# Inputs of the next block as separate tasks, low parts of the FFN on VectorE, early banks that change roles, and a longer Sinkhorn step

## The chip, the cores and the metric

The kernel runs on one core of a Trainium2 chip. The metric is the device time of one execution in microseconds; lower is better. TensorE (PE) does the matmuls, VectorE (DVE), ScalarE (ACT) and GpSimd (POOL) the elementwise work, and SyncE (SP) issues nearly all DMAs.

## What is computed

Three stages, all in float32: attention with a local mask in four heads and a strided mask in the other four, then a mixture of experts whose gate is normalised by eight Sinkhorn rounds, then an FFN with a sigmoid activation.

```python
scores = scale * q @ k.T                # 4 x 8 heads, 576 tokens, 64 wide
attn = softmax(where(mask, scores, -1e9))
x = (attn @ v) as (2304, 512)
P = exp(x @ w_gate - max)               # 8 experts
for _ in range(8):
    P /= P.sum(1, keepdims=True) + 1e-9
    P /= P.sum(0, keepdims=True) + 1e-9
    P *= N / E
for e in range(8):
    out += P[:, e:e+1] * (max(x @ w1[e], 0) @ w2[e])    # 512 -> 1024 -> 512
h = out @ w_in                          # 512 -> 2048
y = (h * sigmoid(1.702 * h)) @ w_out    # 2048 -> 512
```

## The kernel before

**Precision.** Every float32 operand of the large matmuls is split into a high part (rounded by a copy on ACT) and a low part (the difference), and a product is the sum of high x high, low x high and high x low: three matmuls in the fast fp32r form.

**Blocks, units, pieces.** The 2304 tokens are three blocks of 768. `PHASES` (line 145) gives the order of the passes: moe block 0, moe 1, FFN 0, moe 2, FFN 1, FFN 2. A pass consists of units (`UNITS`), each a slice of 256 hidden columns: 32 units for a moe pass, 8 for an FFN pass, 120 in all; they are numbered 0 to 119. In a unit the up projection is done by the seven products of a Strassen scheme (`PRODUCTS`, line 39) instead of eight: the inputs are X11, S1, S2, X12, S3, S4, X22, where S1 to S4 are sums of quarters of the block's input. Each product is six matmuls of 384 columns and accumulates in PSUM banks A, B and C. The down projection of the unit before is six tiles (`tile_down`) of six matmuls of 512 columns. The work is emitted in pieces that alternate: product 0, down tile 0, product 1, down tile 1, and so on; the last product (X22) has no tile behind it. A unit has 13 pieces (`PPU`), and piece k of unit i is `piece_at(i, k)`; product m is piece 2m. Small tasks are hung behind pieces in the table `side`. The order is written out by hand, and each engine runs its own instructions in that order.

**After the products** (`product_and_after`, `activate`, lines 580 to 632). ACT copies partial sums out of a bank, DVE adds them to another bank, and each of four quarters "11", "22", "12", "21" is activated. In the moe ACT writes the high part hh with a Relu, and DVE writes the low part hl (line 589). In the FFN ACT computes the sigmoid (594), DVE multiplies (595), ACT copies to hh (596), and POOL writes the low part hl (599). The low part is returned as `rest` and called behind the next down tile (`after`); only for the last quarter, "21", it is called at once while the attention is still running. The down tile needs hh in its first two and hl in its third matmul (lines 646 to 648). Its result y is added to the accumulator on DVE (lines 659 to 675).

**Banks.** While the attention runs (`late` is empty), A, B and C have one bank each, as the attention holds the others; the last products of a unit (X22) and the first of the next one (X11) both use A. From `early.close()` on each of the three has two banks in turn (`open_bank`, line 117). Units 0 to about 8 run between the steps of the attention; the first piece starts at about 71 us.

**Inputs of a block** (`combine`, line 292; `plan_inputs`, line 320). For each of the seven products of the next pass it issues, where there is one, the sum S1 to S4, then ACT's copy to the high part (316) and the low part (317). Product 0's is issued in the last unit but one of the pass before (behind its piece 8), product m's behind piece 2m - 1 of the last unit. Sums and low parts run on POOL, for a pass over block 0 on DVE. S1 and S3 share one buffer, S2 and S4 another, and S2 is computed from S1, S4 from S2. The tiles xc have eight buffers, one more than a pass needs.

**Weights.** For passes over block 0 (units 0 to 31 and 64 to 71) the weights of each unit are summed on POOL (`sums_w1`, 185 to 187) and split by ACT and POOL (`split_w1`, 204, 205; `split_w2`, 217, 218) one unit ahead, and kept in DRAM; the other passes load them split. POOL is free of that work there. The FFN weights are decoded from 64-bit words on DVE and POOL (`decode`, 254 to 266) as side tasks between the gate and unit 60.

**Gate.** The first twelve units (three experts) don't wait for the gate: their outputs are parked in DRAM and joined later by DVE (line 689), from unit 14 on. The gate's steps (`gate_steps`, line 545) are hung behind consecutive pieces once the attention has been issued: each of eight iterations is a row half on DVE (`sinkhorn_rows`, which ends with the partial column sums, 532), an empty step, and a column half (`sinkhorn_cols`), which begins with a matmul over partitions on PE (536) and goes on on DVE.

Of the kernel before, what the change touches and what calls it, by code (L numbers as in the profile page):

```python
# [8 lines left out]
F32 = mybir.dt.float32  # L9
F32R = mybir.dt.float32r  # L10
U32 = mybir.dt.uint32
AF = mybir.ActivationFunctionType
ALU = mybir.AluOpType
AX = mybir.AxisListType

P = 128
# [9 lines left out]
NH = 384  # L26
BT = 2 * NH
# [11 lines left out]
PRODUCTS = (  # L39
    ("X11", "W11", "A", True, False),  # L40
    ("S1", "T1", "C", True, False),
    ("S2", "T2", "A", False, False),
    ("X12", "W21", "B", True, True),
    ("S3", "T3", "A", False, False),
    ("S4", "W22", "C", False, True),
    ("X22", "T4", "A", False, True),
)
# [4 lines left out]
def strided_attention_moe_ffn(  # L52
# [13 lines left out]
    nc = tc.nc  # L66
    B, NPAIR, _, _, S = qk.shape
# [20 lines left out]
    stp = ctx.enter_context(tc.tile_pool(name="stp", bufs=1))  # L88
# [6 lines left out]
    ps = ctx.enter_context(tc.tile_pool(name="ps", bufs=1, space=bass.MemoryType.PSUM))  # L95
# [17 lines left out]
    late = []  # L113
    bank = {}
    turn_of = defaultdict(int)

    def open_bank(b):
        turn_of[b] += 1
        pool, tag = (late[0], b + "2") if late and turn_of[b] % 2 else (ps, b)
        bank[b] = pool.tile([P, 512], F32, tag=tag, name="p" + b)  # L120
        return bank[b]

# [8 lines left out]
    def f(t):  # L131
        return t.bitcast(F32)


    side = defaultdict(list)
# [9 lines left out]
    PHASES = [("moe", 0), ("moe", 1), ("ffn", 0), ("moe", 2), ("ffn", 1), ("ffn", 2)]  # L145
# [11 lines left out]
    def piece_at(unit, k):  # L157
        return unit * PPU + k
# [130 lines left out]
    xc = {}  # L289
    xin = {}  # L290

    def combine(ph, m):

        x = xin[ph]
        X11, X12 = x[:, 0:2, 0:NH], x[:, 2:4, 0:NH]
        X21, X22 = x[:, 0:2, NH:BT], x[:, 2:4, NH:BT]
        if ("sa", ph) not in xin:
            xin["sa", ph] = stp.tile([P, 2, NH], F32, tag="sa", name="sa")
            xin["sb", ph] = stp.tile([P, 2, NH], F32, tag="sb", name="sb")
        sa, sb = xin["sa", ph], xin["sb", ph]  # L300

        v = nc.gpsimd if ph and PHASES[ph][1] else nc.vector
        what = PRODUCTS[m][0]
        if what == "S1":
            v.tensor_tensor(out=sa, in0=X21, in1=X22, op=ALU.add)
        elif what == "S2":
            v.tensor_tensor(out=sb, in0=sa, in1=X11, op=ALU.subtract)
        elif what == "S3":
            v.tensor_tensor(out=sa, in0=X11, in1=X21, op=ALU.subtract)
        elif what == "S4":  # L310
            v.tensor_tensor(out=sb, in0=X12, in1=sb, op=ALU.subtract)
        src = {"X11": X11, "X12": X12, "X22": X22, "S1": sa, "S2": sb, "S3": sa, "S4": sb}[what]
        if ph == 0 and not xc:
            xc.update({(0, n): xcp.tile([P, 2, 2, NH], F32R, tag="xc", name="xc") for n in range(NPR)})
        t = xc[0, m] if ph == 0 else xcp.tile([P, 2, 2, NH], F32R, tag="xc", name="xc")
        nc.scalar.activation(out=t[:, 0], in_=src, func=AF.Copy)  # L316
        v.tensor_tensor(out=t[:, 1], in0=src, in1=f(t[:, 0]), op=ALU.subtract)  # L317
        xc[ph, m] = t

    def plan_inputs():  # L320
        for ph in range(1, len(PHASES)):
            last = FIRST_UNIT[ph] - 1
            side[piece_at(last, 0) - 5].append(lambda ph=ph: combine(ph, 0))
            for m in range(1, NPR):
                side[piece_at(last, 2 * m - 1)].append(lambda ph=ph, m=m: combine(ph, m))


    xblk = [tok.tile([P, KD, BT], F32, tag="tok", name="x") for _ in range(NB)]
# [146 lines left out]
    for n, p in enumerate(pairs):  # L475
        if n > 0:
            i = at[pairs[n - 2]][-1] if n > 1 else -1
# [18 lines left out]
    def gate_logits(blk):  # L496

        pl = spare_bank([P, TB, Q], "pl")
        xv = xblk[blk].rearrange("p k (t c q) -> p k c t q", c=P // Q, q=Q)
        for k in range(KD):  # L500
            for c in range(P // Q):
                nc.tensor.matmul(
                    out=pl[c * Q : (c + 1) * Q],
                    lhsT=wgr[:, k, :],
                    rhs=xv[:, k, c],
                    start=(k == 0),
                    stop=(k == KD - 1),
                )
        lt = stp.tile([P, TB * Q], F32, tag="sg", name="lt", bufs=2)
        nc.vector.transpose(lt, pl.rearrange("p t q -> p (t q)"))  # L510
        nc.vector.tensor_copy(pr[:, blk * TB : (blk + 1) * TB, :], lt.rearrange("p (t q) -> p t q", q=Q)[:, :, :E])
# [33 lines left out]
    def gate_steps():  # L545
        steps = [lambda blk=blk: gate_logits(blk) for blk in range(1, NB)] + [gate_max]
        steps += [lambda: None] * 3 + [gate_exp]
        for _ in range(SINKHORN):
            steps += [sinkhorn_rows, lambda: None, sinkhorn_cols]
        return steps  # L550


# [4 lines left out]
    def product(i, k):  # L557
        ph, kind, blk, n = UNITS[i]
        _, _, b, opens, ends = PRODUCTS[k]
        if opens:  # L560
            open_bank(b)
        o = bank[b][:, :NH]
        w, x = w1.pop((i, k)), xc[ph, k]
        todo = [(kk, hw, hx) for kk in range(2) for hw, hx in ((0, 0), (0, 1), (1, 0))]
        for m, (kk, hw, hx) in enumerate(todo):
            nc.tensor.matmul(  # L566
                out=o,
                lhsT=w[:, hw, kk * P : (kk + 1) * P],
                rhs=x[:, hx, kk, :],
                start=opens and m == 0,  # L570
                stop=ends and m == len(todo) - 1,
                skip_group_check=True,
            )

    def copy_of(b):
        t = cp.tile([P, NH], F32, tag="c", name="c")
        nc.scalar.activation(out=t, in_=bank[b][:, :NH], func=AF.Copy)  # L577
        return t

    def activate(i, q, src):  # L580

        hh = hp.tile([P, NH], F32R, tag="hh" + q, name="hh" + q, bufs=2 if q == "22" else 1)
        hl = hp.tile([P, NH], F32R, tag="hl" + q, name="hl" + q, bufs=2 if q == "22" else 1)
        hid[i, q] = (hh, hl)
        if UNITS[i][1] == "moe":
            nc.scalar.activation(out=hh, in_=src, func=AF.Relu)  # L586

            def rest():
                nc.vector.scalar_tensor_tensor(  # L589
                    out=hl, in0=src, scalar=0.0, in1=f(hh), op0=ALU.max, op1=ALU.subtract  # L590
                )
        else:
            sg = stp.tile([P, NH], F32, tag="sg", name="sg", bufs=2)
            nc.scalar.activation(out=sg, in_=src, func=AF.Sigmoid, scale=1.702)
            nc.vector.tensor_tensor(out=sg, in0=src, in1=sg, op=ALU.mult)
            nc.scalar.activation(out=hh, in_=sg, func=AF.Copy)  # L596

            def rest():
                nc.gpsimd.tensor_tensor(out=hl, in0=sg, in1=f(hh), op=ALU.subtract)  # L599

        return rest

    def add(t, b, to):
        o = bank[to][:, :NH]
        nc.vector.tensor_tensor(out=o, in0=bank[b][:, :NH], in1=t, op=ALU.add)  # L605
        return o

    def product_and_after(i, k):

        product(i, k)  # L610
        x = PRODUCTS[k][0]
        if x == "X11":
            snap["a"] = copy_of("A")
        elif x == "S1":
            snap["c"] = copy_of("C")
        elif x == "S2":
            snap["u"] = copy_of("A")
        elif x == "X12":
            return activate(i, "11", add(snap["a"], "B", "B"))
        elif x == "S3":  # L620
            if late:
                o = open_bank("B")[:, :NH]
                nc.vector.tensor_tensor(out=o, in0=bank["A"][:, :NH], in1=snap["c"], op=ALU.add)
                return activate(i, "22", o)
            return activate(i, "22", add(snap["c"], "A", "B"))
        elif x == "X22":
            rest = activate(i, "21", bank["A"][:, :NH])
            if late:
                return rest
            rest()  # L630
        elif x == "S4":
            return activate(i, "12", add(snap["u"], "C", "C"))

# [113 lines left out]
    with tc.manual_schedule():  # L747
# [19 lines left out]

        plan_weights()
        plan_inputs()
        plan_kept()  # L770
        plan_turns()
# [45 lines left out]
        dp = ctx.enter_context(tc.tile_pool(name="dp", bufs=1, reuse_waits="tile"))  # L817
        g = done[0]
        steps = gate_steps()
        assert g + len(steps) + 2 < piece_at(WAITING * UPE + 1, 0), (g, len(steps))  # L820
        for n, s in enumerate(steps):
# [85 lines left out]
```

## Time and profile before

| | before |
|---|---|
| device time, median of 3 runs | 2095.91 us (2093.35 to 2096.3) |
| the profiled execution: its own time | 2096.66 us |
| its span, first to last instruction | 2094.9 us |
| PE busy | 2028.2 us, 97% |
| DVE busy | 1254.8 us, 60% |
| ACT busy | 707.6 us, 34% |
| POOL busy | 699.4 us, 33% |
| mean granted TensorE clock | 0.989 of 2.4 GHz |

Busy shares are means over stages with different loads. A matmul is recorded with a modelled end, so PE's busy time is an upper figure; what a stage loses is better seen in the distance between like pieces of the chain of waits and in the waits by name. In a windows row the columns are the stretch and its length, the busy time of each engine with its number of instructions, the granted clock, the share of the DMA engines and their rate.

### The profile page before, as it was taken

What the parts mean: (1) busy time and instruction counts of PE and PEld (TensorE: products, weight loads), DVE (VectorE), ACT (ScalarE), POOL (GpSimd) and SP (SyncE); (2) the same over time, 40 slices, a digit from 0 to 9 for tenths busy, and PEclk for the clock granted to TensorE, in tenths of its full rate; (3) what the DMA queues carried; (4) which work ended last, traced back from release to release, by engine and by line L of the source; (5) the groups of instructions that cost most, each with busy time, mean ns of one, the idle gap of its engine ahead of it and who ended that gap; (6) DMA issues with size and microseconds to landing.
All of it is one profiled execution on the core that took longest, in us unless ns stands there. A gap on an engine that the chain in (4) does not pass through costs nothing.

```text
span 2094.9 us, 30326 instructions
## 1 busy us (share of the span) xinstructions
PE 2028.2 (97%) x10538; PEld 1781.8 (85%) x10538; DVE 1254.8 (60%) x2214; ACT 707.6 (34%) x1735; POOL 699.4 (33%) x705
## 2 busy tenths in 40 slices
PE   9799989999998999999999998999999999999899
PEld 6577778888887888888988897798888888898788
DVE  6766577888776666666665643444544545544444
ACT  5555434344443222222222554222222222333332
POOL 3555547777776000000000688100000000423522
PEclk9899999999999999999999999999999999999999
DMA  5467558888886667667666575566556566556553
GB/s 180 154 207 269 203 206 303 313 300 306 290 291 213 206 212 219 207 223 223 215 214 195 202 249 203 191 181 197 177 180 199 178 179 198 172 178 184 172 190 132
DMA packets 185289, 445.52 MB, mean 213 GB/s; under 512 B 21040, under 2 KB 21168, under 8 KB 184368
## 3 DMA queue, kind: packets, MB, share of 16 engines
q1 hardware_dynamic: 184848, 443.12, 64.1%
q8 instruction: 84, 1.38, 0.3%
q14 instruction: 69, 0.57, 0.1%
q10 hardware_dynamic: 288, 0.46, 0.1%
HBM read 310.33 MB, written 133.17 MB: 212 GB/s over the span
## 4 chain that ended last, share of the span: by engine, by line
PE 85%; DVE 6%; POOL 5%; issue 2%; ACT 1%; DMA 1%; POOLq 0%; SPq 0%; DVEq 0%; ACTq 0%
PE pA L566 21%; PE y L648 15%; PE y L646 14%; PE y L647 14%; PE pC L566 11%; PE pB L566 5%; POOL xc L317 1%; PE sc L365 1%; PE idle_out L755 1%; PE av L434 1%; DVE hl L589 1%; POOL w L205 1%; PE pt L416 1%; DVE acc L665 1%; DVE acc L689 1%
## 5 line engine op out<-in xcount | busy, mean ns | idle before, releaser
L665 DVE SCALAR_TENSOR_TENSOR acc<-y,pr,acc 128x512 f32<-128x512 f32 x486 | 364.1, 749 | 445.1 <-PE y L648 442.6
L646 PE MATMUL y<-w,hh 128*128 128x512 f32 x1440 | 569.0, 395 | 22.1 <-ACT hh L596 9.9
L648 PE MATMUL y<-w,hl 128*128 128x512 f32 x1440 | 574.4, 399 | 5.5 <-DVE hl L589 4.4
L566 PE MATMUL pA<-xc,w 128*128 128x384 f32 x2880 | 566.3, 337 | 10.8 <-DVE hl L589 6.1
L647 PE MATMUL y<-w,hh 128*128 128x512 f32 x1440 | 570.5, 396 | 0.0
L566 PEld LDWEIGHTS pA<-xc,w 128*128 128x128 f32 x2880 | 514.2, 189 | 46.2 <-DVE hl L589 7.8
L648 PEld LDWEIGHTS y<-w,hl 128*128 128x128 f32 x1440 | 271.0, 188 | 68.2 <-DVE hl L589 6.7
L646 PEld LDWEIGHTS y<-w,hh 128*128 128x128 f32 x1440 | 271.7, 189 | 62.5 <-ACT hh L596 15.6
L647 PEld LDWEIGHTS y<-w,hh 128*128 128x128 f32 x1440 | 271.2, 188 | 33.7
L566 PE MATMUL pC<-xc,w 128*128 128x384 f32 x1440 | 296.1, 340 | 0.0
L566 PEld LDWEIGHTS pC<-xc,w 128*128 128x128 f32 x1440 | 260.6, 191 | 21.4 <-issue 0.6
L586 ACT ACTIVATE hh<-pB 128x384 fp32r<-128x384 f32 x192 | 94.4, 492 | 395.3 <-DVE pB L605 228.1
L577 ACT ACTIVATE c<-pA 128x384 f32<-128x384 f32 x240 | 117.6, 490 | 258.9 <-PE pA L566 258.9
L265 POOL TENSOR_TENSOR x<-x,r 128x512 f32<-128x512 f32 x32 | 41.4, 1294 | 413.9 <-DVE r L264 392.2
L317 POOL TENSOR_TENSOR xc<-z,xc 128x768 fp32r<-128x768 f32 x6 | 11.1, 1849 | 481.2 <-ACT xc L316 479.1
L599 POOL TENSOR_TENSOR hl<-sg,hh 128x384 fp32r<-128x384 f32 x96 | 97.8, 1019 | 172.1 <-ACT hh L596 148.0
L675 DVE TENSOR_TENSOR acc<-y,acc 128x512 f32<-128x512 f32 x126 | 86.5, 687 | 105.9 <-PE y L648 105.7
L566 PE MATMUL pB<-xc,w 128*128 128x384 f32 x720 | 145.7, 336 | 0.0
L205 POOL TENSOR_TENSOR w<-sums,w 128x256 fp32r<-128x256 f32 x160 | 125.2, 786 | 59.6 <-ACT w L204 52.3
L566 PEld LDWEIGHTS pB<-xc,w 128*128 128x128 f32 x720 | 128.2, 188 | 11.1 <-issue 0.5
L218 POOL TENSOR_TENSOR w<-raw,w 128x512 fp32r<-128x512 f32 x80 | 104.9, 1311 | 78.0 <-ACT w L217 69.4
L577 ACT ACTIVATE c<-pC 128x384 f32<-128x384 f32 x120 | 59.0, 492 | 189.7 <-PE pC L566 189.7
(112 smaller groups left out, 1978.5 us busy)
## 6 DMA issues: line engine op xcount, KB each, us to landing
w<-s1moe SPq DMA_DIRECT2D x448, 256.0 KB, 2.7
w<-s2moe SPq DMA_DIRECT2D x128, 512.0 KB, 3.7
s1moe<-w SPq DMA_DIRECT2D x224, 256.0 KB, 3.3
s2moe<-w SPq DMA_DIRECT2D x64, 512.0 KB, 4.1
w<-s1ffn SPq DMA_DIRECT2D x112, 256.0 KB, 2.7
raw<-wa SPq DMA_DIRECT2D x32, 512.0 KB, 4.6
raw<-wb SPq DMA_DIRECT2D x32, 512.0 KB, 5.4
w<-s2ffn SPq DMA_DIRECT2D x32, 512.0 KB, 3.6
```

The source lines that it names most:

```text
L205: nc.gpsimd.tensor_tensor(out=t[:, 1, :], in0=src, in1=f(t[:, 0, :]), op=ALU.subtract)
L218: nc.gpsimd.tensor_tensor(out=t[:, 1, :], in0=src, in1=f(t[:, 0, :]), op=ALU.subtract)
L265: lambda: nc.gpsimd.tensor_tensor(out=x, in0=x, in1=f(r), op=ALU.add),
L566: nc.tensor.matmul(out=o, lhsT=w[:, hw, kk * P : (kk + 1) * P], rhs=x[:, hx, kk, :], start=opens and m == 0, stop=ends and m == len(todo) - 1,
L577: nc.scalar.activation(out=t, in_=bank[b][:, :NH], func=AF.Copy)
L586: nc.scalar.activation(out=hh, in_=src, func=AF.Relu)
L599: nc.gpsimd.tensor_tensor(out=hl, in0=sg, in1=f(hh), op=ALU.subtract)
L646: nc.tensor.matmul(out=y, lhsT=hh[:, c], rhs=w[:, 0], start=(m == 0), stop=False)
L647: nc.tensor.matmul(out=y, lhsT=hh[:, c], rhs=w[:, 1], start=False, stop=False)
L648: nc.tensor.matmul(out=y, lhsT=hl[:, c], rhs=w[:, 0], start=False, stop=(m == 1))
L665: nc.vector.scalar_tensor_tensor(out=a, in0=y, scalar=p, in1=a, op0=ALU.mult, op1=ALU.add)
L675: nc.vector.tensor_tensor(out=a, in0=y, in1=a, op=ALU.add)
```

## The change

Four edits.

1. `open_bank` takes the unit's number. While the attention runs, A and B change roles in odd units. The low part of quarter "21" is no longer called at once there, but behind the next down tile, as everywhere else.
2. `combine` is divided into `input_sum`, `input_high` and `input_low`, each with the engine as an argument, and `plan_inputs` hangs them apart: S1 and S2 of the next pass behind pieces 6 and 8 of the last unit but one, on POOL; the high part of product 0 behind piece 9 and its low part behind piece 10 of that unit; high and low part of product m behind piece 2m - 1 of the last unit as before; S3 and S4 behind pieces 2 and 4 of the last unit. Before a pass over block 0 (FFN 0) low parts 1, 3, 5 and S3, S4 are on DVE; before the pass that follows one over block 0 (moe 1, moe 2) low parts 0, 3, 6 are on DVE; all others are on POOL. The inputs of pass 0 are made as before.
3. The low part hl of the FFN's activations goes from POOL to DVE.
4. A Sinkhorn iteration has two empty steps between its halves instead of one, so 4 pieces instead of 3; the gate has 39 steps instead of 31, and the decode starts after them.

```diff
-    def open_bank(b):
+    def open_bank(b, i):
         turn_of[b] += 1
-        pool, tag = (late[0], b + "2") if late and turn_of[b] % 2 else (ps, b)
+        pool, tag = ps, b
+        if late and turn_of[b] % 2:
+            pool, tag = late[0], b + "2"
+        elif not late and i % 2:
+            tag = {"A": "B", "B": "A", "C": "C"}[b]
...
+    SUMS = {"S1": "sa", "S2": "sb", "S3": "sa", "S4": "sb"}
+    def input_sum(ph, m, eng):
...
+        what = PRODUCTS[m][0]
         if what == "S1":
-            v.tensor_tensor(out=sa, in0=X21, in1=X22, op=ALU.add)
+            eng.tensor_tensor(out=sa, in0=q["X21"], in1=q["X22"], op=ALU.add)
...
+    def input_high(ph, m):
...
+        nc.scalar.activation(out=t[:, 0], in_=input_of(ph, m), func=AF.Copy)
         xc[ph, m] = t
+    def input_low(ph, m, eng):
+        t = xc[ph, m]
+        eng.tensor_tensor(out=t[:, 1], in0=input_of(ph, m), in1=f(t[:, 0]), op=ALU.subtract)
...
     def plan_inputs():
+        v, g = nc.vector, nc.gpsimd
         for ph in range(1, len(PHASES)):
             last = FIRST_UNIT[ph] - 1
-            side[piece_at(last, 0) - 5].append(lambda ph=ph: combine(ph, 0))
+            shared = PHASES[ph][1] == 0
+            low_v = (1, 3, 5) if shared else (0, 3, 6) if PHASES[ph - 1][1] == 0 else ()
...
+            put(last - 1, 6, input_sum, ph, 1, g)
+            put(last - 1, 8, input_sum, ph, 2, g)
+            put(last - 1, 9, input_high, ph, 0)
+            put(last - 1, 10, input_low, ph, 0, v if 0 in low_v else g)
             for m in range(1, NPR):
-                side[piece_at(last, 2 * m - 1)].append(lambda ph=ph, m=m: combine(ph, m))
+                put(last, 2 * m - 1, input_high, ph, m)
+                put(last, 2 * m - 1, input_low, ph, m, v if m in low_v else g)
+                if m in (1, 2):
+                    put(last, 2 * m, input_sum, ph, m + 3, v if shared else g)
...
-            steps += [sinkhorn_rows, lambda: None, sinkhorn_cols]
+            steps += [sinkhorn_rows, lambda: None, lambda: None, sinkhorn_cols]
...
             def rest():
-                nc.gpsimd.tensor_tensor(out=hl, in0=sg, in1=f(hh), op=ALU.subtract)
+                nc.vector.tensor_tensor(out=hl, in0=sg, in1=f(hh), op=ALU.subtract)
...
         elif x == "X22":
-            rest = activate(i, "21", bank["A"][:, :NH])
-            if late:
-                return rest
-            rest()
+            return activate(i, "21", bank["A"][:, :NH])
```

## Rows read from the trace of the kernel before

**Rows 1.** Page: span; busy time of each engine, share, instructions.

```profile
span 2094.9 us, 30326 instructions
PE 2028.2 (97%) x10538; PEld 1781.8 (85%) x10538; DVE 1254.8 (60%) x2214; ACT 707.6 (34%) x1735; POOL 699.4 (33%) x705
```

**Rows 2.** Chain of waits in order of time: start us, us, what.

```profile
624.46 2.08 PE pA L566 x12
...
679.52 2.08 PE pA L566 x12
...
1152.44 2.08 PE pA L566 x12
...
1188.96 2.08 PE pA L566 x12
...
1269.88 2.08 PE pA L566 x12
...
1330.85 2.08 PE pA L566 x12
...
1800.05 2.08 PE pA L566 x12
...
1832.78 2.08 PE pA L566 x12
...
1929.34 2.08 PE pA L566 x12
...
1972.15 2.08 PE pA L566 x12
```

**Rows 3.** Waits by name, whole span: who waited for whom, us, times, longest.

```profile
ACT xc L316 <- POOL sa L309: 18.2, 4, 6.2
...
PE y L646 <- ACT hh L586: 8.2, 3, 6.2
```

**Rows 4.** Waits of PE and of its weight loads, 95 to 265 us.

```profile
PE pA L566 <- DVE hl L589: 6.1, 8, 1.2
...
PEld pA L566 <- DVE hl L589: 7.8, 8, 1.5
```

**Rows 5.** Waits of PE, 265 to 325 us.

```profile
PE pc L536 <- DVE sk L532: 6.2, 6, 2.1
```

**Rows 6.** Busy time in four stretches: Sinkhorn, moe 0, FFN 0, moe 2.

```profile
280.00:322.00 42.00, 35.83 (x172) 30.43 (x171) 34.86 (x100) 13.11 (x33) 23.16 (x27) 0.96 0.62 225
...
531.00:640.00 109.00, 109.00 (x545) 97.93 (x544) 79.05 (x127) 47.09 (x113) 81.84 (x87) 1.00 0.82 282
...
1190.00:1271.00 81.00, 81.00 (x416) 72.90 (x416) 38.99 (x66) 45.65 (x106) 70.50 (x81) 1.00 0.71 244
...
1332.00:1785.00 453.00, 453.00 (x2261) 407.11 (x2260) 227.66 (x377) 99.87 (x203) 0.00 (x0) 1.00 0.60 187
```

**Rows 7.** Groups by line: shapes, count | busy us, mean ns | idle before.

```profile
L599 POOL TENSOR_TENSOR hl<-sg,hh 128x384 fp32r<-128x384 f32 x96 | 97.8, 1019 | 172.1 <-ACT hh L596 148.0 <-PE pA L566 23.9
...
L218 POOL TENSOR_TENSOR w<-raw,w 128x512 fp32r<-128x512 f32 x80 | 104.9, 1311 | 78.0 <-ACT w L217 69.4 <-DVE pB L623 8.5
...
L317 POOL TENSOR_TENSOR xc<-sb,xc 128x768 fp32r<-128x768 f32 x8 | 14.9, 1863 | 7.6 <-ACT xc L316 7.6
...
L316 ACT ACTIVATE xc<-sb 128x768 fp32r<-128x768 f32 x12 | 10.1, 843 | 33.7 <-POOL sb L311 13.0 <-POOL sb L307 12.2 <-DVE sb L311 5.0
...
L595 DVE TENSOR_TENSOR sg<-pB,sg 128x384 f32<-128x384 f32 x48 | 26.7, 557 | 45.7 <-ACT sg L594 45.0 <-POOL w L205 0.6
...
L317 DVE TENSOR_TENSOR xc<-x,xc 128x768 fp32r<-128x768 f32 x3 | 2.9, 958 | 1.9 <-ACT xc L316 1.8
...
L311 DVE TENSOR_TENSOR sb<-x,sb 128x768 f32<-128x768 f32 x1 | 3.7, 3694 | 0.0
```

**Rows 8.** Groups of DVE by line, 531 to 640 us (moe 0).

```profile
L264 DVE SCALAR_TENSOR_TENSOR r<-r,u 128x512 f32<-128x512 uint32 x5 | 4.4, 871 | 0.0
```

**Rows 9.** Groups of DVE by line, 762 to 1138 us (moe 1).

```profile
L264 DVE SCALAR_TENSOR_TENSOR r<-r,u 128x512 f32<-128x512 uint32 x15 | 10.2, 682 | 0.0
```

More of the change, by code (lines that the diff above doesn't have):

```diff
@@ L290, in strided_attention_moe_ffn, with quarters, input_of @@
     xin = {}
-    def combine(ph, m):
+    SUMS = {"S1": "sa", "S2": "sb", "S3": "sa", "S4": "sb"}
+    def quarters(ph):
         x = xin[ph]
-        X11, X12 = x[:, 0:2, 0:NH], x[:, 2:4, 0:NH]
-        X21, X22 = x[:, 0:2, NH:BT], x[:, 2:4, NH:BT]
+        return {"X11": x[:, 0:2, 0:NH], "X12": x[:, 2:4, 0:NH], "X21": x[:, 0:2, NH:BT], "X22": x[:, 2:4, NH:BT]}
+    def input_sum(ph, m, eng):
+        q = quarters(ph)
         if ("sa", ph) not in xin:
-            xin["sa", ph] = stp.tile([P, 2, NH], F32, tag="sa", name="sa")
-            xin["sb", ph] = stp.tile([P, 2, NH], F32, tag="sb", name="sb")
+            for n in ("sa", "sb"):
+                xin[n, ph] = stp.tile([P, 2, NH], F32, tag=n, name=n)
         sa, sb = xin["sa", ph], xin["sb", ph]
-        v = nc.gpsimd if ph and PHASES[ph][1] else nc.vector
         what = PRODUCTS[m][0]
         if what == "S1":
-            v.tensor_tensor(out=sa, in0=X21, in1=X22, op=ALU.add)
+            eng.tensor_tensor(out=sa, in0=q["X21"], in1=q["X22"], op=ALU.add)
         elif what == "S2":
-            v.tensor_tensor(out=sb, in0=sa, in1=X11, op=ALU.subtract)
+            eng.tensor_tensor(out=sb, in0=sa, in1=q["X11"], op=ALU.subtract)
         elif what == "S3":
-            v.tensor_tensor(out=sa, in0=X11, in1=X21, op=ALU.subtract)
+            eng.tensor_tensor(out=sa, in0=q["X11"], in1=q["X21"], op=ALU.subtract)
         elif what == "S4":
-            v.tensor_tensor(out=sb, in0=X12, in1=sb, op=ALU.subtract)
-        src = {"X11": X11, "X12": X12, "X22": X22, "S1": sa, "S2": sb, "S3": sa, "S4": sb}[what]
+            eng.tensor_tensor(out=sb, in0=q["X12"], in1=sb, op=ALU.subtract)
+    def input_of(ph, m):
+        what = PRODUCTS[m][0]
+        return xin[SUMS[what], ph] if what in SUMS else quarters(ph)[what]
+    def input_high(ph, m):
         if ph == 0 and not xc:
@@ L315, in combine, with put @@
         t = xc[0, m] if ph == 0 else xcp.tile([P, 2, 2, NH], F32R, tag="xc", name="xc")
-        nc.scalar.activation(out=t[:, 0], in_=src, func=AF.Copy)
-        v.tensor_tensor(out=t[:, 1], in0=src, in1=f(t[:, 0]), op=ALU.subtract)
+        nc.scalar.activation(out=t[:, 0], in_=input_of(ph, m), func=AF.Copy)
         xc[ph, m] = t
+    def input_low(ph, m, eng):
+        t = xc[ph, m]
+        eng.tensor_tensor(out=t[:, 1], in0=input_of(ph, m), in1=f(t[:, 0]), op=ALU.subtract)
+    def combine(ph, m):
+        input_sum(ph, m, nc.vector)
+        input_high(ph, m)
+        input_low(ph, m, nc.vector)
     def plan_inputs():
+        v, g = nc.vector, nc.gpsimd
         for ph in range(1, len(PHASES)):
             last = FIRST_UNIT[ph] - 1
-            side[piece_at(last, 0) - 5].append(lambda ph=ph: combine(ph, 0))
+            shared = PHASES[ph][1] == 0
+            low_v = (1, 3, 5) if shared else (0, 3, 6) if PHASES[ph - 1][1] == 0 else ()
+            def put(unit, k, fn, *args):
+                side[piece_at(unit, k)].append(lambda: fn(*args))
+            put(last - 1, 6, input_sum, ph, 1, g)
+            put(last - 1, 8, input_sum, ph, 2, g)
+            put(last - 1, 9, input_high, ph, 0)
+            put(last - 1, 10, input_low, ph, 0, v if 0 in low_v else g)
             for m in range(1, NPR):
-                side[piece_at(last, 2 * m - 1)].append(lambda ph=ph, m=m: combine(ph, m))
+                put(last, 2 * m - 1, input_high, ph, m)
+                put(last, 2 * m - 1, input_low, ph, m, v if m in low_v else g)
+                if m in (1, 2):
+                    put(last, 2 * m, input_sum, ph, m + 3, v if shared else g)
     xblk = [tok.tile([P, KD, BT], F32, tag="tok", name="x") for _ in range(NB)]
@@ L560, in product @@
         if opens:
-            open_bank(b)
+            open_bank(b, i)
         o = bank[b][:, :NH]
@@ L621, in product_and_after @@
             if late:
-                o = open_bank("B")[:, :NH]
+                o = open_bank("B", i)[:, :NH]
                 nc.vector.tensor_tensor(out=o, in0=bank["A"][:, :NH], in1=snap["c"], op=ALU.add)
```

## The prediction, made before the changed kernel was run

> **What bounds the kernel now.** I read the head of the page first [rows 1]. The span is 2094.9 us and the timed run of that execution 2096.66 us, so 1.76 us lie outside the span; the median of the runs is 2095.91 us, 0.75 us below it. PE is busy 97% and no other engine over 60%. PE sets the time, so the change is worth what it gives back of PE's waits and of the stretches at the half clock behind them.
>
> Next I read the chain of waits in order of time [rows 2]. A piece "pA x12" is the last product of a unit and the first of the next one, back to back, 2.08 us; it comes once a unit. In the undisturbed stretch from 1330.85 to 1800.05 it recurs 30 times, every 469.20 / 30 = 15.64 us. That is the floor of a unit, and a product takes 2.08 / 2 = 1.04 us of it, a down tile (15.64 - 7 x 1.04) / 6 = 1.39 us. What a stretch takes above the floor is lost, and the same rows show where. Moe block 0 to 1: 679.52 - 624.46 = 55.06 us for 3 units, 8.1 lost. Moe 1 to FFN 0: 36.52 for 2 units, 5.2 lost. FFN 0 to moe 2: 60.97 for 3 units, 14.1 lost. Moe 2 to FFN 1: 32.73 for 2 units, 1.5 lost. FFN 1 to FFN 2: 42.81 for 2 units, 11.5 lost. Together **40.4 us at five changes of block**, half-clock time included.
>
> The waits by name [rows 3] say why: at the changes PE waits for ACT's hh, by up to 6.2 us at once, and ACT's copy of the new inputs waits for POOL's sums. ACT works in order, so the activations of the old block stand behind the copies of the new one. Two smaller losses lie earlier. In 95 to 265 us PE waits 8 times for the low part of the hidden tile before the first product of a unit, 6.1 us on PE and 7.8 us on the weight load in front of it [rows 4]. In 280 to 322 us PE waits 6 times for the Sinkhorn row half, 6.2 us [rows 5], and that window's clock of 0.96 is 42 x 0.04 = 1.7 us more [rows 6].
>
> **Part 1, early banks.** Until the attention is done, each of A, B and C has one bank. The first product of a unit opens A, which the last product of the unit before has just filled; it waits for the activation and the low part of that. With A and B swapped in odd units it opens the bank of "22", whose low part was queued four pieces earlier. The low part of "21" now goes behind the next unit's first down tile; its bank is wanted next by that unit's fourth product, two down tiles and two products later (about 4.9 us), which hides it. If that cover went, the same 1 us a unit would come back. No instruction is added. Gain: at most 7.8 us, at least 0 (if the attention steps between the pieces, which also need DVE, ACT and POOL, set the pace). I take 7.0, near the upper end, because this is the longest wait of PE in that window: the attention, at its present pace, holds PE up less.
>
> **Part 2, Sinkhorn.** One more piece between a row half and its column half: PE comes to the column matmul 1.04 or 1.39 us later. The six waits are 6.2 us, the longest 2.1 [rows 5], so the longest keeps about 1 us and the five others (0.8 us on average) go or nearly go. But DVE is busy 34.86 of 42 us there [rows 6]. Eight iterations over 32 pieces instead of 24 have the same nine DVE instructions each and a third more time, so DVE is less crowded too, though still not idle. I take 5.5 of 6.2 + 1.7 = 7.9 us, bounds 2 and 7.9. The eight pieces that the gate ends later (about 8 x 1.2 = 9.6 us) have cover: unit 13's pieces use it first, and the code asserts that. The decode's steps move back by those eight pieces and lie about 1% denser, costed at nothing: if one falls on a join of the parked experts it may cost or give about 1 us, in the range.
>
> **Part 3, inputs of the next block.** One block has 11 combining operations: 4 sums and 7 low parts. On POOL each takes about 1.85 us (the row has 1.863); on DVE 0.96 us; ACT's high copy 0.84 us [rows 7]. Before, POOL had 10 of them in the last unit, 18.5 us, and each sum stood in front of the copy that waits for it. In FFN 0's last unit POOL had in addition four low parts of the activations (4 x 1.02 = 4.1) and two splits of w2 (2 x 1.31 = 2.6): 25.2 us in a unit of 15.64. That is a queue of 9.6 us in a place where ACT, and so PE, wait for it.
>
> After, two sums run one unit earlier, S3 and S4 five pieces ahead of their copies, and low parts 0, 3, 6 are on DVE where weights are being split. POOL's last unit is then S3, S4 and four low parts, 6 x 1.85 = 11.1, and 2.6 of splits: 13.7 us, under 15.64 (moe 0 to 1 with a decode add of 1.3: 15.0). The unit before takes two sums, 3.7 us. In moe 0 POOL is busy 81.84 of 109 us, 11.7 a unit [rows 6], so 15.4 with them: full, but not over. In FFN 0 it is 70.50 of 81, 13.6 a unit, less 4.1 (part 4) plus 3.7: 13.2. At the two changes where POOL keeps all (to FFN 1, to FFN 2) its last unit has 8 x 1.85 = 14.8 us, and the activations' low parts no longer stand behind them. A low part that is late costs nothing for some 14 pieces: it is queued at piece 2m - 1 of the last unit and its product is piece 2m of the next. At moe 1 to FFN 0, where DVE did all 11 (11 x 0.96 = 10.6 us on top of a moe unit), it keeps 5, 4.8 us. A moe unit without decode has DVE at 227.66 of 453 us, 7.9 us [rows 6], so 12.7 instead of 18.5: the wait is gone.
>
> Moved past: the copies on ACT keep their places but the first, one piece later; no DMA moves, and SP's queue is untouched. The new low parts on DVE wait for ACT's copy of the same piece, with the next accumulations queued behind; the copy (0.84) runs beside the down tile (1.39), so the wait is short. I leave 3 us of the 40.4, about half a microsecond a change, for copies that get in front of an activation: gain 37.4, bounds 20 (half the queue stays) and 40.4.
>
> **Part 4, low parts of the FFN's activations on DVE.** 96 instructions leave POOL (1019 ns each) and enter DVE. The nearest DVE row of that size, the product sg, takes 557 ns [rows 7], but reads one input from PSUM; the new one reads both from SBUF. Two-input instructions on DVE took 871 ns with POOL at 75% and 682 ns in moe 1, where POOL has little to do [rows 8, 9], so I take 0.56 + 0.19 = 0.75 us in FFN 0. DVE's load there is 38.99 of 81 us, 7.5 a unit [rows 6]; with 4 x 0.75 = 3.0 it is 10.5 of 15.64. It is free in the steady units, where FFN units already run at 15.64 outside the stretch of the transposes. Its use is in part 3, where POOL's queue gets shorter.
>
> The bound from above is the worst DVE row, one sum of 3694 ns, beside low parts of the same size at 0.96 [rows 7]. The Trainium skill, SBUF — State Buffer, section "Who interferes with whom", states that a VectorE instruction with two SBUF inputs and a GpSimd one that reads SBUF lock each other out for whole instructions; rows 8 and 9 agree that such instructions get longer beside a busy POOL, by 0.19 us on average and not by a whole instruction each time. By that rule at its hardest the sum would be the second rival's 2061 us.
>
> **Sum.** 2096.66 - 7.0 - 5.5 - 37.4 = 2046.8, **about 2047 us**. Bounds: all gains 7.8 + 7.9 + 40.4 = 56.1, 2040.6; all at the low end 0 + 2 + 20 = 22, 2074.7.
>
> **Rivals.** First, the early stage is paced by the attention and the gate by DVE: parts 1 and 2 give nothing and only the block changes do, 2096.66 - 37.4 = 2059 us. For it: DVE is 83% busy in the Sinkhorn stretch. Against: PE's waits there are for one instruction each.
>
> Second, DVE waits for a whole POOL instruction each time. A low part costs 0.56 + 1.31 = 1.87 us in FFN 0, still 7.5 + 7.5 = 15.0 a unit and free; but in the last unit of a block 1.85 us is added to each combining operation: FFN 0's 7.5 + 7.5 + 2 x 2.81 = 20.6, 5 us over, and moe 1's 7.9 + 5 x 2.81 = 21.9, 6.3 over, and some 3 us at moe 0. That is the rule of the Trainium skill's page SBUF — State Buffer taken to its end. It gives 2047 + 14 = 2061 us.
>
> Third, on the other side: the FFN 0 block becomes DVE-bound. If every low part took the 3.69 us of the worst row, a unit had 7.5 + 4 x 3.69 = 22.3 us on DVE, 6.7 over, times 8 units 53 us: 2100 us, slower than before. It costs from (15.64 - 7.5) / 4 = 2.0 us each and decides the sign where 32 of them eat the 49.9 us gained, 49.9 / 32 = 1.6 more, at about 3.6 us each. Against it: that row is a single instruction, and the two-input ones beside a busy POOL average 0.87 us [rows 8].
>
> Fourth, the sums are early but ACT still holds the activations back behind the copies, so half of the 40.4 us stays: 2096.66 - 12.5 - 20.2 = 2064 us.
>
> **How the numbers follow.** Forecast 0.62, first rival 0.14, second 0.12, fourth 0.07, third 0.03; 0.02 is left for effects that cancel. The range takes the full gains less the scatter of the runs (about 3 us), 2038, up to the fourth rival and a little of the low bound, 2068. A measurement of this kernel can tell about 0.2% (4 us) from no change. Faster 0.95, same 0.02, slower 0.03.
>
> **What would show it.** Right: five "pA x12" intervals at the block changes near multiples of 15.64; no wait of ACT's input copies for POOL's sums over 1 us; no wait of PE for hh over 1 us there; the eight waits before first products gone; the clock full from 100 us on; low parts of the FFN on DVE at 0.56 us beside an idle POOL and about 0.75 in FFN 0. Wrong: new waits of PE for DVE's hl or acc in FFN 0, transposes that wait in the early stage for as long as the first products did, Sinkhorn waits that stay.

## The result, and the profile after

| | before | after |
|---|---|---|
| device time, median | 2095.91 us (3 runs, 2093.35 to 2096.3) | 2060.59 us (4 runs, 2058.31 to 2064.13) |
| ratio after / before | | 0.9836, 95% interval 0.9816 to 0.9857 |
| the profiled execution: its own time, span | 2096.66, 2094.9 us | 2064.13, 2062.3 us |
| DVE busy | 1254.8 us | 1310.8 us |
| POOL busy | 699.4 us | 608.1 us |

The change gives 35.3 us, 1.6%. A fourth execution of before took 3300.2 us and is left out of its median. The forecast was 2047 us, a gain of 49.9 from the 2096.66 us of the profiled execution. The profiled execution of after is the longest of its four, so what its trace loses is at the upper end. This is the head of its page; the lines answer to [rows 1].

```profile
span 2062.3 us, 30239 instructions
...
PE 2023.6 (98%) x10538; PEld 1778.3 (86%) x10538; DVE 1310.8 (64%) x2310; ACT 705.4 (34%) x1735; POOL 608.1 (29%) x609
```

The chain of waits of after in order of time (start us, us, what) has the same piece as [rows 2]: the last product of a unit and the first of the next. Shown are the pairs around the five changes of block.

```profile
621.35 2.08 PE pA L601 x12
...
669.56 2.08 PE pA L601 x12
...
1142.46 2.08 PE pA L601 x12
...
1190.27 2.08 PE pA L601 x12
...
1255.55 2.08 PE pA L601 x12
...
1310.12 2.08 PE pA L601 x12
...
1779.32 2.08 PE pA L601 x12
...
1810.60 2.08 PE pA L601 x12
...
1907.16 2.08 PE pA L601 x12
...
1939.20 2.08 PE pA L601 x12
```

Against units of 15.64 us: moe 0 to 1 takes 48.21 us for 3 units, 1.3 lost (before 8.1); moe 1 to FFN 0 47.81 for 3, 0.9 lost (5.2); FFN 0 to moe 2 54.57 for 3, **7.7 lost** (14.1); moe 2 to FFN 1 31.28 for 2, nothing (1.5); FFN 1 to FFN 2 32.04 for 2, 0.8 lost (11.5). Of 40.4 us 10.6 are left, most of it at one change.

PE's waits in 265 to 345 us show the gate. The answer for before is [rows 5].

```profile
PE y L678 <- DVE acc L693: 3.8, 1, 3.8
PE pc L571 <- DVE sk L567: 2.1, 3, 1.2
PE pA L601 <- ACT c L612: 1.7, 1, 1.7
```

The Sinkhorn waits fell from 6.2 to 2.1 us, but the first line is new: a down tile waits for an accumulation on DVE, once, for 3.8 us. The timeline of that place (start, us, engine, line, operation, in brackets the idle time before it) shows what DVE was waiting for.

```profile
321.93 0.58 SPq L259 DMA_DIRECT2D w<-wc  x1
...
328.80 0.43 DVE L260 TENSOR_SCALAR u<-w 128x512 uint32<-128x512 uint32 x1 [6.90 <-DMA s1moe<-w]
329.14 0.68 DVE L693 TENSOR_TENSOR acc<-y,acc 128x512 f32<-128x512 f32 x1
...
329.88 0.50 PE L678 MATMUL y<-w,hh 128*128 128x512 f32 x1 [3.79 <-DVE acc L693]
```

The first decode instruction on DVE (line 260) reads the tile w, whose load was issued at 321.93 and is first used at 328.80. DVE stands 6.90 us, the accumulations stand behind it in its queue, and PE, which needs a bank of y that they have read, stops. The releaser's name is that of another DMA on the queue; line 260 reads only w, and issuing the load earlier removes the wait (below). From 322 to 329 us the DMA engines were busy 99% of the time.

At FFN 0 to moe 2 the groups of DVE by line, 1262 to 1300 us (count | busy us, mean ns | idle), show what got dearer:

```profile
L634 DVE TENSOR_TENSOR hl<-sg,hh 128x384 fp32r<-128x384 f32 x8 | 7.3, 915 | 0.1
L332 DVE TENSOR_TENSOR xc<-x,xc 128x768 fp32r<-128x768 f32 x3 | 6.8, 2260 | 0.0
```

The three low parts of moe 2's inputs took 2.26 us on average on DVE (1.66, 2.55 and 2.57), where [rows 7] have 0.96. PE's waits there, 1262 to 1310 us:

```profile
PE y L678 <- ACT hh L631: 2.1, 1, 2.1
PE y L680 <- DVE hl L634: 1.9, 2, 1.3
```

### The profile page after: what moved, and what is told of

It reads as the page before. It is cut to its first block, busy times and chain, and to the rows that moved or that the text cites. A ratio compares the mean times of both kernels' runs of the same rounds, so it can differ in the third digit from the quotient of the medians.

```text
span 2062.3 us, 30239 instructions
## 1 busy us (share of the span) xinstructions
PE 2023.6 (98%) x10538; PEld 1778.3 (86%) x10538; DVE 1310.8 (64%) x2310; ACT 705.4 (34%) x1735; POOL 608.1 (29%) x609
## 4 chain that ended last, share of the span: by engine, by line
PE 87%; DVE 6%; issue 2%; DMA 2%; ACT 1%; POOL 1%; POOLq 0%; ACTq 0%; SPq 0%; DVEq 0%
PE pA L601 22%; PE y L680 15%; PE y L678 15%; PE y L679 15%; PE pC L601 11%; PE pB L601 5%; DMA acc<-kept 1%; PE sc L400 1%; PE idle_out L787 1%; PE av L469 1%; PE pt L451 1%; DVE acc L697 1%; POOL w L210 1%; DVE hl L634 1%; DVE xc L332 1%
## 5 line engine op out<-in xcount | busy, mean ns | idle before, releaser
L621 ACT ACTIVATE hh<-pC 128x384 fp32r<-128x384 f32 x96 | 47.2, 492 | 180.6 <-DVE pC L640 176.4
```

## The experiments

The first four take the kernel before and make one part of the change each; the others start from the changed kernel or from one of these. Each ran with the kernel before beside it, whose median lay between 2095.26 and 2096.68 us. The changed kernel was timed once, with the result, so a difference from its 2060.59 us carries that scatter of 1.4 us.

### Part 1 alone

```diff
-        pool, tag = (late[0], b + "2") if late and turn_of[b] % 2 else (ps, b)
+        pool, tag = ps, b
+        if late and turn_of[b] % 2:
+            pool, tag = late[0], b + "2"
+        elif not late and i % 2:
+            tag = {"A": "B", "B": "A", "C": "C"}[b]
...
-            rest = activate(i, "21", bank["A"][:, :NH])
-            if late:
-                return rest
-            rest()
+            return activate(i, "21", bank["A"][:, :NH])
```

> The kernel before with part 1 alone (A and B change roles, low part of quarter 21 behind the next down tile). Theory: the eight waits before first products go and units 0 to 8 give back 6.5 us, as they did with all parts together, so about 2089.5 us and no more waits of pA for hl in 95 to 265 us. Rival (attention paces the early stage): 2096 us, the waits move to the transposes or scores.

Measured: 2089.22 us beside 2095.26, 0.9971 (0.9962 to 0.9980), **6.0 us faster**. Of PE's waits in 95 to 265 us these are the longest two; the eight waits of [rows 4] are gone and nothing took their place in that window.

```profile
PE pt L420 <- ACT hh L590: 0.6, 1, 0.6
PE pt L420 <- DVE x L448: 0.6, 3, 0.2
```

The attention did not set the pace. Behind that window PE's Sinkhorn waits (265 to 345 us) are 7.2 us, the longest 3.2, where [rows 5] have 6.2 and 2.1: about 1 us of the gain is lost again there.

### Part 2 alone

```diff
-            steps += [sinkhorn_rows, lambda: None, sinkhorn_cols]
+            steps += [sinkhorn_rows, lambda: None, lambda: None, sinkhorn_cols]
```

> The kernel before with part 2 alone (four pieces per Sinkhorn iteration). In the changed kernel units 9 and 10 gave back 4.5 us and unit 11 lost 6.3 us to a wait of DVE for the first decode load. Theory A (the load is late because the decode begins eight pieces later, at a crowded place of the DMA queue): units 9 and 10 give 4.5, unit 11 loses about 6, net 2096 to 2098 us. Theory B (the load is late because PE is ahead of the DMAs there, through parts 1 and 2 together): unit 11 loses little with part 2 alone, 2091.5 us.

Measured: 2100.93 us, 1.0029 (1.0018 to 1.0041): alone, part 2 makes the kernel **5.7 us slower**, more than theory A had. PE's waits in 265 to 345 us:

```profile
PE y L646 <- DVE acc L661: 4.0, 1, 4.0
PE pA L566 <- ACT c L577: 2.2, 1, 2.2
PE pc L536 <- DVE sk L532: 1.8, 2, 1.2
```

The Sinkhorn waits fall from 6.2 to 1.8 us, and the wait for an accumulation is there with part 2 alone. So the late load comes from part 2 and not from PE being ahead; theory B falls. DVE's wait for that load, in 265 to 345 us, first in the kernel before and then with part 2, shows what part 2 does to it:

```profile
DVE u L255 <- DMA w<-wc: 2.7, 1, 2.7
```

```profile
DVE u L255 <- DMA w<-wc: 7.1, 1, 7.1
```

The kernel before has the wait too, but no down tile is held up by its 2.7 us ([rows 5] are all that PE waits there).

### Part 3 alone

The functions `input_sum`, `input_high`, `input_low` and the new `plan_inputs`, as in the diff above; the FFN's low parts stay on POOL.

> The kernel before with part 3 alone (inputs of the next block as separate tasks; the FFN's low parts stay on POOL). The changed kernel gave back 29.8 of 40.4 us at the five block changes. Theory A (part 4 is needed, since POOL's last unit is full without it): FFN 0 to moe 2 has 17.8 us on POOL and FFN 1 to FFN 2 18.9, so 2 to 3 us more are lost at each than in the changed kernel, 25 us given back in all, 2071 us. Theory B (what is left at FFN 0 to moe 2 is contention that part 4 brings): less is lost there than the 7.6 us of the changed kernel, 31 us or more given back, 2065 us or less.

Measured: 2067.31 us, 0.9868 (0.9854 to 0.9883), **28.0 us faster**, between the two numbers expected. FFN 0 to moe 2, in the chain of waits, takes 56.85 us for 3 units, 9.9 lost:

```profile
1257.61 2.08 PE pA L596 x12
...
1314.46 2.08 PE pA L596 x12
```

With all parts it is 7.7. PE waits 6.1 us at this change, in two waits, for POOL's low parts of the activations. The other four changes lose 1.2, 0.4, 0.0 and 1.3 us. Beside part 3, part 4 lowers the loss at this change by some 2 us; theory A in kind, with a smaller size.

### Part 4 alone

```diff
-                nc.gpsimd.tensor_tensor(out=hl, in0=sg, in1=f(hh), op=ALU.subtract)
+                nc.vector.tensor_tensor(out=hl, in0=sg, in1=f(hh), op=ALU.subtract)
```

> The kernel before with part 4 alone (low parts of the FFN's activations on DVE). Theory A: POOL's queue at FFN 0 to moe 2 and at FFN 1 to FFN 2 gets 4.1 us shorter and the losses there fall by 3 to 4 us each, 2088 us. Theory B (contention with POOL eats it in FFN 0): only FFN 1 to FFN 2 gains, 2092 us. Theory C (DVE-bound, the third rival of the prediction): FFN 0's units take more than 15.64 us each and the time is over 2096 us.

Measured: 2088.05 us, 0.9963 (0.9949 to 0.9978), **7.2 us faster**: theory A. The chain of waits has the gain at the two places named:

```profile
1283.62 2.08 PE pA L566 x12
...
1324.97 2.08 PE pA L566 x12
...
1907.85 2.08 PE pA L566 x12
...
1963.14 2.08 PE pA L566 x12
```

FFN 0 to moe 2 takes 41.35 us for 2 units, 10.1 lost (before 14.1); FFN 1 to FFN 2 55.29 for 3, 8.4 lost (11.5): 4.0 and 3.1 us.

The four parts alone give 6.0 - 5.7 + 28.0 + 7.2 = 35.5 us, and together 35.3. That the sums agree is chance, for the parts do not act alone: beside part 3, part 4 lowers the loss at the five changes from about 13 to 10.6 us in the traces, not by 7.2, and beside the others part 2 costs 2.2 us by the medians, not 5.7 (below).

### The first decode load eight pieces earlier

The changed kernel, with one task moved; the decode's other steps stay.

```diff
-            if i == 0:
-                order.append((0, 0))
...
+        side[lo - 8].append(lambda: step(0, 0))
```

> The changed kernel with one edit: the load of the first decode chunk is issued eight pieces earlier, all else of the decode stays. Theory A (DVE's wait for that load in unit 11 is all that part 2 costs): the wait of 6.9 us on DVE and the 4 us stall of PE behind it go, and the half clock behind that, 6.3 us less, 2054 us. Rival (the DMA queue is full there, and an earlier load only delays the weights behind it): the stall moves, 2058 us or more.

Measured: **2053.9 us**, 0.9798 (0.9783 to 0.9812), 6.7 us less than the changed kernel, as theory A had it. Two lines of its timeline, SP's and DVE's:

```profile
310.38 0.48 SPq L259 DMA_DIRECT2D w<-wc  x1
...
320.89 0.42 DVE L260 TENSOR_SCALAR u<-w 128x512 uint32<-128x512 uint32 x1
```

The load is issued 11.55 us earlier and DVE doesn't wait for it. PE's wait for the accumulation is gone too; its waits in 265 to 345 us are now 2.5 us for the Sinkhorn rows, 2.0 for ACT's copy c and 0.2.

### Part 2 with the earlier load, on the kernel before

> The kernel before with part 2 and the first decode load eight pieces earlier. Theory A (part 2 lost only through the late load): units 9 and 10 keep the 4.2 us that part 2 gave alone, unit 11 loses under 1.5 us, so 2091 to 2092 us, where part 2 alone has 2100.9. Theory B (the decode meets the joins and the block changes worse from its new place): 2095 us or more.

Measured: 2090.15 us beside 2095.57, 0.9976 (0.9966 to 0.9986), **5.4 us faster**. Theory A. The longest of PE's waits in 265 to 345 us:

```profile
PE pc L535 <- DVE sk L531: 2.1, 3, 1.2
PE pA L565 <- ACT c L576: 2.0, 1, 2.0
```

One task's place turns part 2 from 5.7 us slower to 5.4 faster: the late load cost about 11 us there. Like products of the two traces tell where. With the late load they come 6.6 us later at 356 us, just behind the wait of 4.0 us named above, 8.4 us later at the end of moe 0 (625.24 against 616.85), 10.2 behind the change to moe 1 and 10.7 at the end. So most of it is lost at the stall, and the rest in the remainder of moe 0, where the joins lie, and at the first change of block. What the decode's steps hold up there is not shown.

### The changed kernel without part 2

> The changed kernel without part 2 (three pieces per Sinkhorn iteration again). If the four parts simply add, as part 2 alone made the kernel before 5.7 us slower, this has 2055 us: units 9 and 10 lose the 4.5 us that part 2 gave, unit 11 gets its 6.3 back, and the decode meets the changes of block otherwise. Rival (part 2 is needed once PE is ahead through part 1): 2061 us or more.

Measured: 2058.4 us, 0.9817 (0.9801 to 0.9834), between the two numbers expected: 2.2 us faster than with part 2 and not 5.7. The interval overlaps that of the changed kernel, so even these 2.2 us are not clear. PE's waits in 265 to 345 us have one line:

```profile
PE pc L571 <- DVE sk L567: 6.6, 5, 3.2
```

Without part 2 the Sinkhorn waits are 6.6 us again, the longest 3.2 instead of 2.1. With its load in time part 2 gives 4.5 us here (2058.4 to 2053.9), with the late load it gives nothing or costs a little.

### Moe 2's low parts on POOL

```diff
-            low_v = (1, 3, 5) if shared else (0, 3, 6) if PHASES[ph - 1][1] == 0 else ()
+            low_v = (1, 3, 5) if shared else (0, 3, 6) if ph == 1 else ()
```

> The changed kernel with the three low parts of moe 2's inputs on POOL instead of DVE. In the changed kernel they took 1.66, 2.55 and 2.57 us on DVE instead of 0.96, beside a POOL without gaps, and FFN 0 to moe 2 still loses 7.6 us. Theory A (that contention is what is left): 3 to 5 us less lost there, 2056 us. Theory B (POOL's queue decides): POOL has 6 x 1.85 + 2.6 + 2 x 1.85 = 17.4 us in the last unit and the loss grows by 2 us or more, 2063 us.

Measured: 2057.59 us, 0.9815 (0.9801 to 0.9830), 3.0 us less than the changed kernel's median, with overlapping intervals, so the place in the trace has to decide. The change from FFN 0 to moe 2 in the chain of waits, and the window 1240 to 1310 us (busy time of PE, weight load, DVE, ACT, POOL; granted clock), first of this kernel:

```profile
1271.15 2.08 PE pA L601 x12
...
1304.24 2.08 PE pA L601 x12
```

```profile
1240.00:1310.00 70.00, 68.93 (x344) 61.04 (x343) 44.54 (x70) 34.50 (x73) 49.33 (x39) 1.00 0.69 234
```

and then of the changed one:

```profile
1240.00:1310.00 70.00, 66.07 (x314) 57.76 (x313) 46.99 (x69) 32.91 (x70) 44.19 (x36) 0.95 0.61 210
```

33.09 us for 2 units, **1.8 lost instead of 7.7**, at full clock. The 7.7 is no accident of one execution: the traces of the earlier load and of the kernel without part 2, which leave this place as it is, have 7.6 each. POOL has 17.4 us of work in the last unit of 15.64 and nobody waits for it. Theory A; theory B falls, and with it the rule of my sum that POOL's last unit has to be under 15.64 us. A low part of an input is due 14 pieces after it is queued, so POOL may be late with it; what hurt at this place was DVE held up.

### FFN 1's sums held back

```diff
+            early0 = ph == 4
+            put(last - 1, 4 if early0 else 9, input_high, ph, 0)
+            put(last - 1, 5 if early0 else 10, input_low, ph, 0, v if 0 in low_v else g)
             put(last - 1, 6, input_sum, ph, 1, g)
             put(last - 1, 8, input_sum, ph, 2, g)
-            put(last - 1, 9, input_high, ph, 0)
-            put(last - 1, 10, input_low, ph, 0, v if 0 in low_v else g)
```

> The changed kernel with product 0 of FFN 1's inputs ahead of its two sums, so that POOL can't run these sums as soon as it is free (they ran 30 units early, at 1292.8 and 1294.7 us, in the middle of the change from FFN 0 to moe 2, and DVE's instructions beside them took 1.62 and 2.57 us instead of 0.56 and 0.96). Theory A: the loss there falls by 1 to 2 us, and if the half clock of 6.8 us behind it goes, by 3 more: 2056 to 2059 us. Theory B (the stall that decides came before these sums): 2060.5 us.

Measured: 2058.91 us, 0.9820 (0.9805 to 0.9834), 1.7 us less than the changed kernel, again within the intervals.

```profile
1253.66 2.08 PE pA L602 x12
...
1304.74 2.08 PE pA L602 x12
```

```profile
1240.00:1310.00 70.00, 66.60 (x331) 58.79 (x330) 44.94 (x69) 33.46 (x71) 38.54 (x33) 1.00 0.65 226
```

51.08 us for 3 units, 4.2 lost instead of 7.7, and the window's clock is 1.00, not 0.95. Theory A: the sums that POOL ran 30 units early were part of the loss, and the half clock behind the stall (70 x 0.05 = 3.5 us) is of the size of that part. The timelines have the same two instructions of DVE, first in the changed kernel, where POOL runs these sums from 1292.8 to 1296.7 us, and then here, where it runs nothing:

```profile
1293.36 1.62 DVE L634 TENSOR_TENSOR hl<-sg,hh 128x384 fp32r<-128x384 f32 x1
1294.91 2.57 DVE L332 TENSOR_TENSOR xc<-x,xc 128x768 fp32r<-128x768 f32 x1
```

```profile
1291.47 0.56 DVE L635 TENSOR_TENSOR hl<-sg,hh 128x384 fp32r<-128x384 f32 x1
1292.20 0.96 DVE L332 TENSOR_TENSOR xc<-x,xc 128x768 fp32r<-128x768 f32 x1 [0.18 <-ACT xc L327]
```

So it is POOL's work beside them that makes these instructions long.

### Both, and all three

The earlier load and moe 2's low parts on POOL:

> The changed kernel with the earlier decode load and moe 2's low parts on POOL, without holding FFN 1's sums back. Theory A (the early sums matter only beside low parts on DVE): the same as with all three edits within 1 us. Theory B (they also stretch the activations' low parts on DVE): 1 to 2 us slower than with all three.

Measured: **2046.13 us** beside 2096.68, 0.9765 (0.9749 to 0.9781). With FFN 1's sums held back as well:

> The changed kernel with three edits together: first decode load eight pieces earlier, moe 2's low parts on POOL, FFN 1's product 0 ahead of its sums. If each acts in its own place (unit 11 and the joins; the change from FFN 0 to moe 2), the gains add as far as they don't overlap: 2060.6 - 6.7 for the load, - 3 to 6 for the change, 2048 to 2051 us, and less than 2 us lost at that change. If the load's gain was partly chance of the joins, 2053 us.

Measured: 2046.32 us, 0.9762 (0.9747 to 0.9777), 1.7 us below the range expected. The change from FFN 0 to moe 2 loses 1.8 us in both. The two are equal, theory A: once no input low parts of moe 2 are on DVE, the early sums cost nothing that these runs can tell. The version with two edits is 14.5 us faster than the changed kernel and beats each edit alone.

### FFN 0's low parts of the activations back on POOL

```diff
-                nc.vector.tensor_tensor(out=hl, in0=sg, in1=f(hh), op=ALU.subtract)
+                e = nc.gpsimd if UNITS[i][2] == 0 else nc.vector
+                e.tensor_tensor(out=hl, in0=sg, in1=f(hh), op=ALU.subtract)
```

on top of the version with two edits.

> The changed kernel with the earlier load and moe 2's low parts on POOL, and with the low parts of FFN 0's activations back on POOL (FFN 1 and FFN 2 keep theirs on DVE). In FFN 0 they took 0.69 us on average on DVE and 0.56 in FFN 1. Theory A (in FFN 0 part 4 is worth POOL's queue, not DVE's time): POOL has 17.4 + 4.1 = 21.5 us in the last unit, the change from FFN 0 to moe 2 loses 4 to 8 us more than the 1.8 without this edit, 2050 to 2054 us. Theory B (contention on DVE is worth as much): 2046 us or less.

Measured: 2054.23 us, 0.9804 (0.9789 to 0.9819), 8.1 us slower. PE's waits in 1240 to 1310 us have one line, and the change takes 40.79 us for 2 units, 9.5 lost:

```profile
PE y L680 <- POOL hl L634: 6.4, 2, 4.4
```

```profile
1259.91 2.08 PE pA L600 x12
...
1300.70 2.08 PE pA L600 x12
```

A low part of an activation is due within a few pieces; behind POOL's input work it comes up to 4.4 us late. Theory A, at the upper end of its 2050 to 2054 us.

## Why the prediction was right, and where it was not

The sign and the range held: 2060.6 us lies in 2038 to 2068. The point was 13.6 us too low; from the kernel before, 49.9 us forecast and 35.3 measured. Two terms make up the difference: the late load of part 2, 6.7 us by the earlier load, and the low parts of moe 2's inputs on DVE, 7.8 more by moving these to POOL as well. With both edits the kernel takes 2046.1 us, where the forecast was 2047; that it comes so near is in part luck, as parts 1 and 2 gave about 1 us less each than forecast.

**What bounds the kernel**: right. The places read from [rows 2 to 5] are where the time came from. Of the signs named beforehand, three of the right ones failed: one change of five is 7.7 us off a multiple of 15.64, PE waits 2.1 us for hh there, and the clock is not full behind the two stalls (0.89 from 329 to 345 us, 0.95 from 1240 to 1310). One of the wrong ones came: PE waits 1.9 us for DVE's hl in that same place.

**Part 1**, 7.0 forecast, 6.0 measured alone. The first rival (attention paces) falls for this part: the waits of [rows 4] were for a bank whose last reader was the low part. The run makes both halves of part 1 at once, the exchanged banks and the later low part, and does not say what each is worth. What is missing to 7.0 has the size of the longer Sinkhorn waits behind it.

**Part 2**, 5.5 forecast, 5.7 slower measured alone. The mechanism was right, and its size nearly: with the load in time it gives 5.4 us on the kernel before and 4.5 beside the other parts. The step that failed is the sentence that the decode's steps move back by eight pieces and are "costed at nothing". I had looked at how dense they lie and not at the first of them: a DMA with one step between its issue and the DVE instruction that reads it, and accumulations queued behind that one. "No DMA moves" stands under part 3 and is true of that part only; part 2 moves this one. Its price was 10.8 us on the kernel before and 6.7 in the changed one. The load should have been named as the thing that is moved past, with SP's queue and the time to land as its price.

**Part 3**, with part 4, 37.4 forecast; the losses at the five changes fall by 29.8 us in the traces, from 40.4 to 10.6. Sums ahead did what was said: in the trace of after ACT's input copies wait for POOL's sums nowhere ([rows 3] have 18.2 us for one of the sums); the three such waits left, 1.9 to 3.3 us, are for DVE's sums of pass 0. The 3 us that were to be left over were 10.6 in the profiled execution, and 7.7 of them lie at FFN 0 to moe 2. The term that was mis-sized is the input low part on DVE beside a POOL without gaps: 0.96 us in the sum, 2.26 measured. That is the second rival's mechanism (0.96 + 1.85 = 2.81 us, 5 over in FFN 0's last unit). It came at moe 0 to 1 as well, where only 1.3 us are lost:

```profile
L332 DVE TENSOR_TENSOR xc<-x,xc 128x768 fp32r<-128x768 f32 x3 | 4.9, 1647 | 0.0
```

At moe 1 to FFN 0, where it should have cost 6.3 us, the three low parts on DVE took 0.94 to 1.14 us, and 0.9 is lost. The Trainium skill, SBUF — State Buffer, section "Who interferes with whom", has a VectorE instruction with two SBUF inputs contend with a GpSimd instruction that reads SBUF, and calls what they contend for an exclusive lock. The low part of 2.57 us beside POOL's sums and 0.96 without them agrees with that; no run shows which of the two engines held the other, or why so little was added at moe 1 to FFN 0.

My condition for POOL, its last unit under 15.64 us, was the wrong one. POOL with 17.4 us costs little when the surplus is low parts of inputs (1.8 lost), and POOL with the activations' low parts in the queue as well, 21.5 us, costs 9.5. What counts is which item in the queue is due first.

**Part 4**: right in its price. The low parts take 0.556 us on DVE beside an idle POOL (1816 to 1900 us) and 0.691 in FFN 0 (1172 to 1262 us, POOL busy 61.2 of 90), forecast 0.56 and 0.75, first FFN 0:

```profile
L634 DVE TENSOR_TENSOR hl<-sg,hh 128x384 fp32r<-128x384 f32 x23 | 15.9, 691 | 0.3
```

```profile
L634 DVE TENSOR_TENSOR hl<-sg,hh 128x384 fp32r<-128x384 f32 x20 | 11.1, 556 | 0.4
```

PE has no wait from 1172 to 1262 us. The third rival (FFN 0 bound by DVE, 2100 us) falls with it. The fourth (ACT still holds the activations back) falls with the losses of 1.3, 0.9, 0.0 and 0.8 us at four changes. That the time lies near the first rival's 2059 us is chance, and near the second's 2061 largely so: it is a late load and one contended place, and the second rival had three such places and no late load.

## What to carry to other kernels

When a run of side tasks moves, price its first item by itself: a load that is issued one step before its use can stall the engine that reads it and all that is queued behind; here a move of eight pieces cost 10.8 us in one kernel and 6.7 in the other. Sort an overfull queue by when its results are due, not by its sum: here input preparation with a unit of slack could overflow, an activation's low part could not. And try a move to another engine beside the busy engine it shares inputs with: the same instruction took 0.96 us alone and 2.26 on average beside a POOL queue without gaps.

## What the runs showed of the hardware

POOL ran two instructions far ahead of the place they were written at, as nothing in its queue held them. In the changed kernel FFN 1's two sums stand behind pieces of unit 102, and POOL ran them in unit 72, beside the low parts that PE waited for; holding them back gave 3.5 us at that change in the trace and 1.7 us in the median, within the intervals. The clock made a stall into a larger loss: in the changed kernel the window around that change was granted 0.95, so part of it ran at 1.2 GHz behind waits of PE of 2.1 and 1.9 us; without the early sums, with waits of 2.1 and 1.3, it was granted 1.00.

One wait is explained only in part. PE's 1.7 us for ACT's copy at unit 9 is new in after and not in the answer of before. It belongs to part 2: every one of the kernels with part 2 above whose waits are given there has it (1.7 to 2.2 us), and the kernel before, part 1 alone and the changed kernel without part 2 have none; they wait for the Sinkhorn rows in that stretch instead. It lies where POOL, behind the gate's maximum over the partitions, issues nothing for 6.8 us, as the group of its weight splits between 262 and 300 us has it, and ACT's copies of the summed weights, ahead of that copy in its queue, wait 7.2 us for POOL's sums. No run took the maximum off POOL, so this cause is argued and not shown.

```profile
L210 POOL TENSOR_TENSOR w<-sums,w 128x256 fp32r<-128x256 f32 x8 | 5.9, 744 | 8.6 <-issue 6.8 <-ACT w L209 1.7
```
